# Slice 0's long convolution filter transformed earlier, its first shift's last two additions moved to accumulating DMAs, in the backward pass of a gated block

## The chip, the cores and the metric

The kernel runs on 1 core of a Trainium2 chip. A core has a matrix engine (TensorE, PE in the profile), a vector engine (VectorE, DVE), a scalar/activation engine (ScalarE, ACT), a general engine (GpSimd, POOL) and a queue engine (SyncE, SP). DMAs are issued from SP, ACT and POOL, each into a queue of its own, and all run on the core's 16 DMA engines. The metric is the device time of one execution in microseconds (us); lower is better.

## What is computed

The reference runs a forward pass and its gradients with respect to nine inputs. S = 2048 rows, D = 1024 columns, F = 3584.

```python
    def _A_ref(q, k, v, shift_k, ssm_k, ssm_D):
...
        k_pad = jnp.pad(k, ((0, 0), (ks - 1, 0), (0, 0)))
        k_shift = jnp.zeros_like(k)
        for t in range(ks):
            k_shift = k_shift + k_pad[:, t:t + S, :] * shift_k[:, ks - 1 - t][None, None, :]
        kv = k_shift * v
...
        y_f = kv_f * kf_f[None, :, :, :]
        y = (lambda x, s, axes=(-2,-1): jnp.fft.irfft2(x, s=s, axes=axes).astype(jnp.bfloat16))(y_f, (1, L), axes=(1, 2))[:, 0, :S, :]
        y = y + kv * ssm_D[None, None, :]
        return q * y

    def _B_ref(x, w_gate, w_up, w_down):
        g = jnp.einsum("bsd,df->bsf", x, w_gate)
        u = jnp.einsum("bsd,df->bsf", x, w_up)
        h = g * u
        return jnp.einsum("bsf,fd->bsd", h, w_down)

    x = A_q
    xn = _layernorm(x, axis=-1)
    s = _A_ref(xn, A_k, A_v, A_shift_k, A_ssm_k, A_ssm_D)
    g = _silu(_B_ref(xn, B_w_gate, B_w_up, B_w_down))
    return x + s * g
```

The outputs are `out` and the gradients of `sum(out * grad_out)`. Part A is a four-tap causal shift of k, a product with v, and a long causal convolution (by Fourier transforms of length 2S) with the filter `ssm_k`. Part B is a gated linear unit.

## The kernel before

**Stages.** From 0 to about 50 us the rows of x are normalized (six chunks of 1, 1, 2, 4, 4 and 4 row blocks, list `chunks`), transposed into `XNT` and, chunk by chunk, multiplied with the first weight slabs. Until about 500 us the gate and up products of all 14 slabs run on PE (`gu_unit`), and in between the forward convolution of part A. Then follow the down projection, the gate with silu, the backward convolution and the weight gradients.

**A unit of the gate and up products.** `gu_unit(sl, b0, n, w, tick)` (L658) takes one slab of 256 + 256 weight columns and n row blocks. For each block it issues 8 matmuls of 512 columns into a PSUM tile `psg` (L676), a cast by ACT into `gut` (L678), and a call of `tick`. The product of gate and up, `hN`, is made by DVE in the next unit (L687), stored by POOL (`Hd<-hN`) and transposed by PE some blocks later. Slabs are loaded by SP (`load_slab`, L546, two DMAs of 512 KB, L550) into the tile `wslab`, which has two buffers: slab 2 can only be loaded when the last unit of slab 0 is done, slab 3 after slab 1.

**The convolution as a generator.** `conv_forward` (L745) yields the estimated DVE time of each piece. `make_pump` (L469) runs it up to a given share of `F_TOTAL`, and `tick` (L1019) calls the pump after every row block, so that the pieces are spread over the units. It works on 8 slices of 128 columns. Pairs of slices share k and v: `load_kv` (L748) loads them, by POOL, into `krow` and `U[4]`; `shift` (L765) makes the four-tap shift of pair 0 and the product kv, `shift_later` (L784) that of pairs 1 to 3. In `shift` DVE makes 4 products, 3 additions and the product with v, 8 instructions of about 2.3 us. In `shift_later` the 3 additions are DMAs issued by POOL that add `U[7]` to `U[6]` (L794). POOL then stores the shift (`KSHd`).

For slice 0 come, in this order: `shift(0)`, the transposes of the filter rows (`h_rows`, L800), two halves of the filter's transform on PE and ACT (`half`, L848, with `fwd8_half`, L286), the butterflies of the filter's transform on DVE (`transform`, L855, with `fwd8`, L296, in six steps), within them the two halves of kv's transform (`ahead`), the butterflies of kv's transform, their product and the inverse transform. `fwd8(..., late=True)` calls `ahead(0)` after its second and `ahead(1)` after its third step behind the sums.

**Tables.** The transforms multiply with two tables of sines and cosines, `T4[0]` and `T4[1]` (in the tile `TF`). `angles` (L154, POOL) makes the integer angles `m` and `mm`, `mask_angles` (L168, DVE) reduces them, `build_tables` (L175, ACT) makes sine, absolute value and sine for each table, and `turn_tables` (L185) transposes both into the tile `TI`. Slice 0's transforms (`fwd8_half`) read only `T4[0]`; `T4[1]` is first read by `turn_tables`.

**What sets the order.** Instructions are traced in program order and then ordered on each engine by a scheduler, in the order of tracing among those that it takes for ready. An instruction that is ready early can go ahead of others that were traced before it. Two means hold it: `tc.issue_after(x)` queues a block's instructions behind x on x's engine, and `tc.keep_in_program_order` puts an instruction behind everything traced on its engine so far (all DVE instructions made by `tt` and `stt` once `PIN[0]` is set, and the first matmul of each part of a held half transform). The loads of k and v of pair 0 stand in a block behind the row store of chunk 4 (`issue_after(xsts[4].ins)`). On its engine each instruction runs in the order so fixed.

**Where the pieces stand.** The last units of slabs 0 and 1 are written by (slab, chunk): (0,4), (0,5), (1,4), (1,5). The pump starts after (0,5). `cnt` counts blocks from -5: the filter rows are transposed from the first block of (1,4) on (`cnt == -4`), the filter's halves and the rest from its third block on (`cnt >= -2`).

Of the kernel before, what the change touches and what calls it, by code (L numbers as in the profile page):

```python
# [19 lines left out]
def build_kernel(  # L20
# [12 lines left out]
    P = 128  # L33
# [120 lines left out]
    def angles(tg):  # L154
# [9 lines left out]
        mm = tg.tile([P, 8, P], I32, name="mm1")  # L164
        E.iota(mm[:], pattern=[[512, 8], [0, P]], base=0, channel_multiplier=0)
        return (m, mm), ins

    def mask_angles(ang):  # L168

        m, mm = ang  # L170
        tt(mm[:], m[:], mm[:], ADD)
        for x in ang:
            V.tensor_single_scalar(x[:], x[:], 4095, ALU.bitwise_and)

    def build_tables(tg, ang):  # L175

        for q, mm in enumerate(ang):
            dst = T4[q].rearrange("p r k f -> p k r f")
            sc = 2.0 * np.pi / 4096.0
            nc.scalar.activation(dst[:, 1], mm[:], ACT.Sin, bias=negpi[:], scale=sc)  # L180
            ab_ = tg.tile([P, 8, P], F32, name="ab_")
            nc.scalar.activation(ab_[:], mm[:], ACT.Abs, bias=negpi[:], scale=sc)
            nc.scalar.activation(dst[:, 0], ab_[:], ACT.Sin, bias=mhpi[:], scale=1.0)
# [555 lines left out]
    SHIFT_W = 8 * 2.3  # L739
# [5 lines left out]
    def conv_forward():  # L745
        S_ = conv_state

        def load_kv(dp, c):  # L748
            S_["k", dp] = krow
            if dp > 1 and c == 0:  # L750
                load_taps(WB[:, :, dp % 2], dp * 256, 256)
            if dp > 0 or c == 0:
                for i in range(2) if dp == 0 else (c,):
                    cld_k(krow[:, i], i, dp)
            if dp > 0 or c == 1:
                for i in range(2) if dp == 0 else (c,):
                    v = U[4][:, 2048 * i:2048 * i + 2048].rearrange("p (a x) -> p a x", a=8)
                    cld_v(v, i, dp * 256, 256)
# [6 lines left out]
        def shift(dp):  # L765
            kv = cx.tile([P, NB, 256], BF16, name="kv")
            S_["kvt", dp] = kv
            k = S_.pop(("k", dp))
            wb = lambda j: WB[:, j:j + 1, dp % 2].unsqueeze(1).to_broadcast([P, 2, 8, 256])
            room = cx.tile([P, 16, 256], BF16, name="KX")[:].rearrange("p a x -> p (a x)") if dp == 0 else U[7][:]  # L770
            acc, prod, v = [t.rearrange("p (c r d) -> p c r d", c=2, r=8) for t in (U[6][:], room, U[4][:])]
            with tc.issue_after(last.ins):
# [1078 lines left out]
```

## Time and profile before

| | us |
|---|---|
| median of 3 runs | 1908.7 (1908.37 to 1909.15) |
| the profiled execution | 1907.69 |
| its span | 1905.9 |
| granted TensorE clock | 1.0 throughout |

The span is the time from the first to the last instruction in the profile. Busy times are of instructions on an engine; matmuls are pipelined, so that their records overlap. Around the change the profile has these times (us from the span's start):

| what | start | end |
|---|---|---|
| last k of pair 0 issued by POOL | 38.7 | |
| v of pair 0 issued, four DMAs | 39.8 | |
| first product of the shift on DVE | 50.03 | 52.3 |
| third addition of the shift | 64.94 | 67.2 |
| product kv | 67.27 | 69.6 |
| table 1 made on ACT (three instructions) | 60.30 | 64.5 |
| k of pair 1 issued from | 65.2 | |
| filter's half transforms on PE | 68.35 | 71.6 |
| filter's sums on DVE | 71.00 | 75.6 |
| filter's third step behind the sums, end | | 83.6 |
| kv's half transforms on PE | 72.97 | 77.2 |
| table transposes on PE, first and second | 89.94 and 101.64 | |

Slab loads to landing took 3.9 to 35.8 us, accumulating DMAs of 1 MB 8.2 to 12.4 us.

### The profile page before, as it was taken

Reading aid. Unit: us, or ns where it says so; the run is one execution under the profiler, and the core shown is the slowest. Engines: PE = TensorE matmul, PEld = TensorE weight load, DVE = VectorE, ACT = ScalarE, POOL = GpSimd, SP = SyncE. Lnnn points to the kernel's source line nnn. Section 1 sums busy time; section 2 is a strip of 40 time slices with the busy share of each in tenths; the row PEclk is TensorE's granted clock in tenths of the full one; section 3 lists DMA queues with packets and bytes.
Section 4 is the critical chain, followed back from the end, with each engine's and each line's share of the span. In section 5 each row is a group of like instructions: output and inputs, shape, how many; then the busy total and the mean of one; then the engine's idle time right before and its main releaser. Section 6 shows DMA issues by size and latency. Waiting matters only on the chain.

```text
span 1905.9 us, 28127 instructions
## 1 busy us (share of the span) xinstructions
PE 1895.9 (99%) x11363; PEld 1012.1 (53%) x11363; DVE 1541.4 (81%) x1726; ACT 636.9 (33%) x928; POOL 348.1 (18%) x479
## 2 busy tenths in 40 slices
PE   8999999999999999999999999999999999999999
PEld 5555555555444466666666655664444444444444
DVE  8999999999977546887999999999995305788872
ACT  5755555555332234332222222222222102011121
POOL 5213122111013210001121221211212101111120
PEclk9999999999999999999999999999999999999999
DMA  9989878888769996677897799585877999899862
GB/s 298 311 249 302 262 243 266 249 284 278 253 219 313 302 328 227 210 231 235 252 283 237 238 252 267 191 283 172 240 230 190 227 201 199 173 185 194 189 182 102
DMA packets 428562, 454.82 MB, mean 239 GB/s; under 512 B 268656, under 2 KB 343692, under 8 KB 414096
## 3 DMA queue, kind: packets, MB, share of 16 engines
q1 hardware_dynamic: 355504, 226.97, 44.7%
q0 software_dynamic: 43936, 184.11, 31.5%
q10 hardware_dynamic: 28992, 41.95, 6.2%
q8 instruction: 89, 1.46, 0.3%
q14 instruction: 41, 0.34, 0.1%
HBM read 194.92 MB, written 189.84 MB: 202 GB/s over the span
## 4 chain that ended last, share of the span: by engine, by line
PE 97%; DVE 1%; ACT 1%; DMA 0%; SPq 0%; issue 0%
PE psb L1538 20%; PE psx L1683 20%; PE psg L676 19%; PE psb L1521 10%; PE psbm L1069 10%; PE psb L1621 9%; PE psF L233 3%; PE psI L454 1%; PE tr L568 1%; PE psY L1228 1%; PE psY L444 1%; PE psx L1621 1%; DVE bst L581 0%; DMA wslab<-in_B_w_gate_dram 0%; PE tr L811 0%; PE psY L1621 0%
## 5 line engine op out<-in xcount | busy, mean ns | idle before, releaser
L676 PE MATMUL psg<-wslab,U 128*128 128x512 bf16 x1792 | 403.0, 379 | 3.4 <-DMA wslab<-in_B_w_gate_dram 2.0
L1538 PE MATMUL psb<-U,U 128*128 128x512 bf16 x1792 | 397.1, 379 | 0.0
L1683 PE MATMUL psx<-U,dgut 128*128 128x512 bf16 x1536 | 332.8, 379 | 0.0
L1683 PEld LDWEIGHTS <-dgut 128*128 128x128 bf16 x1792 | 175.3, 98 | 211.4
L1538 PEld LDWEIGHTS <-U 128*128 128x128 bf16 x1792 | 175.3, 98 | 197.9
L676 PEld LDWEIGHTS <-U 128*128 128x128 bf16 x1792 | 172.0, 98 | 195.7 <-issue 3.6
L1521 PE MATMUL psb<-wdt,U 128*128 128x256 bf16 x1792 | 205.6, 273 | 0.0
L211 DVE TENSOR_TENSOR W<-W 128x1024 f32<-128x1024 f32 (+1 forms) x195 | 191.7, 998 | 4.2
L1521 PEld LDWEIGHTS <-U 128*128 128x128 bf16 x1792 | 175.2, 98 | 29.2
L1621 PE MATMUL psb<-U,U 128*128 128x512 bf16 x816 | 177.3, 379 | 0.0
L1543 ACT CAST wb<-psb 128x512 bf16<-128x512 f32 x112 | 65.6, 586 | 315.4 <-PE psb L1538 310.5
L1288 DVE SCALAR_TENSOR_TENSOR dkp<-dkT,kT 128x1024 bf16<-128x1024 bf16 (+2 forms) x64 | 78.3, 1224 | 100.1 <-DMA dkT<-DKSHd 98.4
L1069 PE MATMUL psbm<-U,ht 128*128 128x512 bf16 x672 | 146.0, 379 | 0.0
L1621 PEld LDWEIGHTS <-U 128*128 128x128 bf16 x912 | 88.9, 98 | 103.1
L1715 ACT ACTIVATE dx_t<-dxn 128x1024 bf16<-128x1024 f32 x15 | 15.9, 1057 | 324.0 <-DVE dxn L211 324.0
L678 ACT CAST gut<-psg 128x512 bf16<-128x512 f32 x144 | 84.4, 589 | 112.2 <-PE psg L676 110.0
L1069 PEld LDWEIGHTS <-ht 128*128 128x128 bf16 x672 | 65.6, 98 | 78.1
L211 DVE TENSOR_TENSOR U<-U,dht 128x2048 bf16<-128x2048 bf16 x56 | 68.3, 1220 | 47.1 <-ACT dht L1523 47.0
L1523 ACT CAST dht<-psb 128x512 bf16<-128x512 f32 x112 | 65.6, 587 | 116.4 <-PE psb L1521 116.4
L66 POOL DMA_DIRECT2D Hd<-hN x54 | 38.8, 719 | 246.7 <-DVE hN L211 243.4
L1662 ACT CAST wbs<-psb 128x512 bf16<-128x512 f32 x51 | 29.9, 586 | 145.4 <-PE psb L1621 137.3
L211 DVE TENSOR_TENSOR W<-SP 128x1024 f32<-128x1024 f32 x64 | 74.3, 1219 | 2.6 <-ACT SP L255 1.2
(266 smaller groups left out, 2351.1 us busy)
## 6 DMA issues: line engine op xcount, KB each, us to landing
U<-GUd SPq DMA_DIRECT2D x28, 1024.0 KB, 9.9
DGd<-U SPq DMA_DIRECT2D x28, 1024.0 KB, 6.8
GUd<-gut ACTq DMA_DIRECT2D x36, 512.0 KB, 7.6
out_dram<-wb SPq DMA_DIRECT2D x112, 128.0 KB, 5.3
U<-Hd SPq DMA_DIRECT2D x14, 1024.0 KB, 5.8
Hd<-hN POOLq DMA_DIRECT2D x54, 256.0 KB, 6.5
HTd<-hT ACTq DMA_DIRECT2D x24, 512.0 KB, 5.5
U<-U POOLq DMA_DIRECT2D x9, 1024.0 KB, 11.7
```

The costliest lines, as they stand in the source:

```text
L211: pinned(V.tensor_tensor(o, a, b, op))
L233: mm = nc.tensor.matmul(ps[:, k].rearrange("p (c d) -> p c d", c=2), T[:, r, k, :], xr[:, r], start=(n == 0), stop=(n == len(rs) - 1 and ( ...
L676: gu_mm[0] = nc.tensor.matmul(ps[:], XNT[q][:, dc, qi * P:(qi + 1) * P], w[:, dc].rearrange("p a f -> p (a f)"), start=(dc == 0), stop=(dc ...
L678: nc.scalar.copy(out=gut[:, :, i], in_=ps[:].rearrange("p (a f) -> p a f", a=2))
L1069: mm = nc.tensor.matmul(ps[:, dh * 512:(dh + 1) * 512], ht(fc)[:, i * P:(i + 1) * P], WD[fc // 4][:, fc % 4, dh * 512:(dh + 1) * 512], sta ...
L1288: ins = V.scalar_tensor_tensor(prod[:].rearrange("p r d -> p (r d)")[:, lo:H], dkT[:, 0, lo:H], 1.0, kT[:, 0, 13 + m + lo:13 + m + H], op0 ...
L1521: nc.tensor.matmul(ps[:, x * SLW:(x + 1) * SLW], DBMT[2 * hf + g][:, dc, (b % 4) * P:(b % 4 + 1) * P], wdt[:, dc, :], start=(dc == 0), sto ...
L1523: nc.scalar.copy(out=dht[:, 2 * e:2 * e + 2].rearrange("p b f -> p (b f)"), in_=ps[:])
L1538: nc.tensor.matmul(ps[:], XN[b // 4][:, b % 4, dc * P:(dc + 1) * P], dgus[b // 8][:, :, b % 8], start=(b == 0), stop=(b == NB - 1))
L1543: nc.scalar.copy(out=wb[:, dc % 2].rearrange("p a f -> p (a f)"), in_=ps[:])
L1621: nc.tensor.matmul(ps, h[:, f, b, :], DBM[b // 4][:, b % 4, dh * 512 + d0:dh * 512 + d0 + w], start=(b == 0), stop=(b == NB - 1))
L1683: nc.tensor.matmul(ps[:, dh * 512:(dh + 1) * 512], t[n][:, f, i * P:(i + 1) * P], WGU[n][:, f, dh * 512:(dh + 1) * 512], start=(n == 0 and ...
```

## The change

- `shift(0)` is replaced by `first_shift` and `first_kv`. DVE makes the four products (into `U[6]`, `KX`, `U[7]` and a buffer of `HX`) and one addition. The third and the fourth product are added into `U[6]` by accumulating DMAs, each in two halves of 512 KB, issued by POOL.
- v of pair 0 is no longer loaded in the block behind chunk 4's row store: `load_v(0)` is called after the first pair of accumulating DMAs.
- The product kv and the store `KSHd[0]` (`first_kv`) are made when the filter's transform calls `ahead(1)`, and both halves of kv's transform behind them; before, the halves stood at `ahead(0)` and `ahead(1)`.
- The next pair's `load_kv` and `shift_later` for slice 0 are traced after the filter's transform (`load_next(0)`).
- `build_tables` becomes `build_table`: table 0 is built where both were built, table 1 behind the filter's half transforms. The angles `mm` and the second `ab_` lie in `TI`.
- The pump starts before unit (0,5). `cnt` starts at -9; the filter rows are transposed after the second block of (0,5), the rest from its fourth block on. `F_TOTAL` and the shift's share (`SHIFT0_W`) are smaller.

```diff
@@ -161,26 +161,24 @@
         m = tg.tile([P, 8, P], I32, name="m")
         ins = E.tensor_tensor(m[:], f2[:].unsqueeze(1).to_broadcast([P, 8, P]),
                               tcol[:].unsqueeze(2).to_broadcast([P, 8, P]), ALU.mult)
-        mm = tg.tile([P, 8, P], I32, name="mm1")
-        E.iota(mm[:], pattern=[[512, 8], [0, P]], base=0, channel_multiplier=0)
-        return (m, mm), ins
+        mm = TI[:, 0].rearrange("p r k f -> p (r k f)").bitcast(I32).rearrange("p (r f) -> p r f", r=8)
+        E.iota(mm, pattern=[[512, 8], [0, P]], base=0, channel_multiplier=0)
+        return (m[:], mm), ins
 
     def mask_angles(ang):
 
         m, mm = ang
-        tt(mm[:], m[:], mm[:], ADD)
+        tt(mm, m, mm, ADD)
         for x in ang:
-            V.tensor_single_scalar(x[:], x[:], 4095, ALU.bitwise_and)
-
-    def build_tables(tg, ang):
-
-        for q, mm in enumerate(ang):
-            dst = T4[q].rearrange("p r k f -> p k r f")
-            sc = 2.0 * np.pi / 4096.0
-            nc.scalar.activation(dst[:, 1], mm[:], ACT.Sin, bias=negpi[:], scale=sc)
-            ab_ = tg.tile([P, 8, P], F32, name="ab_")
-            nc.scalar.activation(ab_[:], mm[:], ACT.Abs, bias=negpi[:], scale=sc)
-            nc.scalar.activation(dst[:, 0], ab_[:], ACT.Sin, bias=mhpi[:], scale=1.0)
+            V.tensor_single_scalar(x, x, 4095, ALU.bitwise_and)
+
+    def build_table(q, mm, ab_):
+
+        dst = T4[q].rearrange("p r k f -> p k r f")
+        sc = 2.0 * np.pi / 4096.0
+        nc.scalar.activation(dst[:, 1], mm, ACT.Sin, bias=negpi[:], scale=sc)
+        nc.scalar.activation(ab_, mm, ACT.Abs, bias=negpi[:], scale=sc)
+        nc.scalar.activation(dst[:, 0], ab_, ACT.Sin, bias=mhpi[:], scale=1.0)
 
     def turn_tables(psp):
 
@@ -736,7 +734,7 @@
     ht_st = [None]
     EIGHT = ((0, 0), (0, 1), (3, 0), (5, 0), (6, 0), (7, 0), (7, 1))
     INV8 = (2, 4, 5, 6, 7)
-    SHIFT_W = 8 * 2.3
+    SHIFT_W, SHIFT0_W = 8 * 2.3, 5 * 2.3
 
     conv_state = {"forward": True, "filters": True}
 
@@ -744,42 +742,52 @@
 
     def conv_forward():
         S_ = conv_state
+
+        def load_v(dp, cs_=(0, 1)):
+            for i in cs_:
+                cld_v(U[4][:, 2048 * i:2048 * i + 2048].rearrange("p (a x) -> p a x", a=8), i, dp * 256, 256)
 
         def load_kv(dp, c):
             S_["k", dp] = krow
             if dp > 1 and c == 0:
                 load_taps(WB[:, :, dp % 2], dp * 256, 256)
-            if dp > 0 or c == 0:
-                for i in range(2) if dp == 0 else (c,):
-                    cld_k(krow[:, i], i, dp)
-            if dp > 0 or c == 1:
-                for i in range(2) if dp == 0 else (c,):
-                    v = U[4][:, 2048 * i:2048 * i + 2048].rearrange("p (a x) -> p a x", a=8)
-                    cld_v(v, i, dp * 256, 256)
+            for i in range(2) if dp == 0 else (c,):
+                cld_k(krow[:, i], i, dp)
+            if dp > 0:
+                load_v(dp, (c,))
 
         def load_h(ds):
             hrow = U[5][:, 0:2048].rearrange("p (c u r) -> p c u r", c=2, r=8)
             cld(U[5][:, 0:2048], A_ssm_k[ds * P:(ds + 1) * P, :])
             S_["h", ds] = hrow
 
-        def shift(dp):
+        def first_shift():
             kv = cx.tile([P, NB, 256], BF16, name="kv")
-            S_["kvt", dp] = kv
-            k = S_.pop(("k", dp))
-            wb = lambda j: WB[:, j:j + 1, dp % 2].unsqueeze(1).to_broadcast([P, 2, 8, 256])
-            room = cx.tile([P, 16, 256], BF16, name="KX")[:].rearrange("p a x -> p (a x)") if dp == 0 else U[7][:]
-            acc, prod, v = [t.rearrange("p (c r d) -> p c r d", c=2, r=8) for t in (U[6][:], room, U[4][:])]
-            with tc.issue_after(last.ins):
-                tt(acc, k[:, :, 0:8, :], wb(3), MUL)
-            yield 2.3
-            for j in (2, 1, 0):
-                tt(prod, k[:, :, 3 - j:11 - j, :], wb(j), MUL)
+            S_["kvt", 0] = kv
+            k = S_.pop(("k", 0))
+            wb = lambda j: WB[:, j:j + 1, 0].unsqueeze(1).to_broadcast([P, 2, 8, 256])
+            rooms = [U[6][:], cx.tile([P, 16, 256], BF16, name="KX")[:].rearrange("p a x -> p (a x)"), U[7][:],
+                     cs.tile([P, 16, 256], BF16, name="HX", bufs=2)[:].rearrange("p a x -> p (a x)")]
+            terms = [t.rearrange("p (c r d) -> p c r d", c=2, r=8) for t in rooms]
+
+            for i, j in enumerate((3, 2, 1, 0)):
+                with tc.issue_after(last.ins) if i == 0 else nullcontext():
+                    tt(terms[i], k[:, :, 3 - j:11 - j, :], wb(j), MUL)
                 yield 2.3
-                tt(acc, acc, prod, ADD)
-                yield 2.3
-            tt(kv[:].rearrange("p (c r) d -> p c r d", c=2), acc, v, MUL)
-            st(KSHd[dp], U[6][:].rearrange("p (b d) -> p b d", b=NB))
-            yield 2.3
+                if i == 1:
+                    tt(rooms[0], rooms[0], rooms[1], ADD)
+                    yield 2.3
+                for c in range(2) if i > 1 else ():
+                    nc.gpsimd.dma_start(out=rooms[0][:, 2048 * c:2048 * c + 2048], in_=rooms[i][:, 2048 * c:2048 * c + 2048],
+                                        accum_op=ADD, max_dma_last_dim=4096)
+                if i == 2:
+                    load_v(0)
+
+        def first_kv():
+            v, acc = [U[i][:].rearrange("p (c r d) -> p c r d", c=2, r=8) for i in (4, 6)]
+            tt(S_["kvt", 0][:].rearrange("p (c r) d -> p c r d", c=2), acc, v, MUL)
+            st(KSHd[0], U[6][:].rearrange("p (b d) -> p b d", b=NB))
+            pe_us[0] -= 2.3 / 0.95
 
         def shift_later(dp):
             kv = cx.tile([P, NB, 256], BF16, name="kv")
@@ -836,8 +844,6 @@
                 yield
 
         load_kv(0, 0)
-        yield 0.0
-        load_kv(0, 1)
         yield 0.0
         cx = pool("cx", 1)
         cs = pool("cs", 1)
@@ -879,7 +885,7 @@
             step()
             yield net(2.4)
 
-        yield from shift(0)
+        yield from first_shift()
         PIN[0] = True
         yield 3.9
         h_rows(0, 0)
@@ -887,13 +893,22 @@
         yield 0.1
         tl = turn_tables(ps_cv)
         sp = [half(0, S_["hx"], i, Dz[:, 0:P]) for i in range(2)]
+        build_table(1, ang[1], TI[:, 1].rearrange("p r k f -> p (r k f)").bitcast(F32).rearrange("p (r f) -> p r f", r=8))
+
+        def first_halves(i):
+            if i == 1:
+                first_kv()
+                sph.extend(half(0, kvs(0), i) for i in range(2))
+
+        def load_next(ds):
+            with tc.issue_after(S_["kst"].ins) if ds else nullcontext():
+                for c in range(2):
+                    load_kv(ds // 2 + 1, c)
+            return shift_later(ds // 2 + 1)
         for ds in range(8):
             yield 0.5
-            if ds % 2 == 0 and ds < 6:
-                with tc.issue_after(S_["kst"].ins) if ds else nullcontext():
-                    for c in range(2):
-                        load_kv(ds // 2 + 1, c)
-                later_kv = shift_later(ds // 2 + 1)
+            if ds in (2, 4):
+                later_kv = load_next(ds)
             D0 = Dz[:, ds * P:(ds + 1) * P]
             sph = []
             KX = cx.tile([P, 16, 256], BF16, name="KX")
@@ -901,7 +916,8 @@
             own_room = lambda X: X[:].rearrange("p a x -> p (a x)").bitcast(F32).rearrange("p (a x) -> p a x", a=8)[:, 0:4]
             eight = (ds, 1) in EIGHT
             if ds == 0:
-                yield from transform(0, 1, sp, HX, own_room(KX), lambda i: sph.append(half(0, kvs(0), i)), nop)
+                yield from transform(0, 1, sp, HX, own_room(KX), first_halves, nop)
+                later_kv = load_next(0)
             else:
                 yield from transform(ds, 0, sp, KX, own_room(HX), lambda i: sph.append(half(ds, S_["hx"], i, D0)), nop)
                 S_["kst"] = st(KFd[ds], KX[:])
@@ -957,7 +973,7 @@
         kst.release()
 
     F_TOTAL = 4 * SHIFT_W + 3.0 + 8 * (0.5 + FWD4_W + 1.3 + PROD_W + INV_W) + 10.0 - 0.95 * 8 * (4 * 1.75 + 0.95 + 4 * 0.9)
-    F_TOTAL -= 3 * 3 * 2.3
+    F_TOTAL -= (3 * 3 + 2) * 2.3
     F_TOTAL += len(EIGHT) * (FWD8_W - 9.6 + 0.95 * 1.75) - 2.0
     F_TOTAL += len(INV8) * (INV8_W - INV_W + 0.95 * 1.8)
     conv = conv_forward()
@@ -994,17 +1010,16 @@
                 spread_taps()
         if i == 3:
             with tc.issue_after(xsts[4].ins):
-                for _ in range(2):
-                    next(conv)
+                next(conv)
         if i == 4:
             with tc.issue_after(act_copy[0].ins):
                 nc.scalar.activation(Dz[0:1, :], Dz[0:1, :], ACT.Copy, scale=WSC)
-        for i_, sl in ([(0, 0)], [(1, 0), (0, 1), (1, 1)], [(2, 0), (2, 1)], [(3, 0), (3, 1)], [(4, 0)], [(5, 0)])[i]:
+        for i_, sl in ([(0, 0)], [(1, 0), (0, 1), (1, 1)], [(2, 0), (2, 1)], [(3, 0), (3, 1)], [(4, 0)], [])[i]:
             gu_unit(sl, *xs[i_][0:2], slabs[sl], nop)
         if i == len(xs) - 1:
             with tc.issue_after(root.ins), tc.issue_after(last.ins):
                 mask_angles(ang)
-                build_tables(tg, ang)
+                build_table(0, ang[0], tg.tile([P, 8, P], F32, name="ab_")[:])
     chunk[0] = len(xs)
     st(RSd.rearrange("(c u r) -> u c r", c=2, u=P), RSTD[:].rearrange("u (c r) -> u c r", c=2))
     st(RSTN[:], RSd.rearrange("(b p) -> p b", p=P))
@@ -1013,19 +1028,19 @@
     ps_st[1].release()
     ps_cv = pool("ps_cv", 2, space=PSUM)
     pump, drain, step = make_pump(conv, F_TOTAL)
-    cnt = [-5]
+    cnt = [-9]
     NT = 24 * 8.0 + 33
 
     def tick(by=1):
         cnt[0] += by
-        if cnt[0] == -4:
-            pump((SHIFT_W + 4.05) / F_TOTAL)
-        if cnt[0] >= -2:
-            pump((SHIFT_W + (F_TOTAL - SHIFT_W) * (cnt[0] + 6.5) / (NT + 3.5)) / F_TOTAL)
-
-    pump((SHIFT_W + 3.95) / F_TOTAL)
-    for i_ in (4, 5):
-        gu_unit(1, *xs[i_][0:2], slabs[1], tick)
+        if cnt[0] == -7:
+            pump((SHIFT0_W + 4.05) / F_TOTAL)
+        if cnt[0] >= -5:
+            pump((SHIFT0_W + (F_TOTAL - SHIFT0_W) * (cnt[0] + 9.5) / (NT + 6.5)) / F_TOTAL)
+
+    pump((SHIFT0_W + 3.95) / F_TOTAL)
+    for sl, i_ in ((0, 5), (1, 4), (1, 5)):
+        gu_unit(sl, *xs[i_][0:2], slabs[sl], tick)
     for sl in range(2, NSL - 2):
         w, wld = load_slab(sl, nc.sync)
         for hf in range(2):
```

## The prediction

> **What bounds the kernel now.** First the page's busy times:
>
> ```profile
> PE 1895.9 (99%) x11363; PEld 1012.1 (53%) x11363; DVE 1541.4 (81%) x1726; ACT 636.9 (33%) x928; POOL 348.1 (18%) x479
> ```
>
> TensorE (PE) works 1895.9 of 1905.9 us. So the sum below only asks which PE waits go and which come. The waits of PE, all of them over 0.2 us in total:
>
> ```profile
> PE psg L676 <- DMA wslab<-in_B_w_gate_dram: 2.0, 2, 1.5
> PE tr L527 <- POOL ident masks.py:199: 1.4, 1, 1.4
> PE psg L676 <- ACT gut L678: 1.1, 2, 0.9
> PE tr L568 <- DVE U L600: 0.7, 1, 0.7
> PE tr L617 <- DVE U L600: 0.5, 1, 0.5
> ```
>
> In the timeline all but 0.2 us of these lie before 40 us (the last at 74.3), ahead of the first instruction that the change reorders on PE. Busy time by stretches confirms it:
>
> ```profile
> 60.00:70.00 10.00, 10.00 (x69) 5.78 (x68) 9.93 (x6) 8.38 (x12) 3.50 (x6) 1.00 0.77 218
> 70.00:80.00 10.00, 9.79 (x63) 5.64 (x61) 9.12 (x11) 9.91 (x14) 5.37 (x7) 1.00 1.02 358
> 80.00:90.00 10.00, 10.00 (x55) 4.79 (x54) 9.90 (x15) 4.28 (x7) 1.37 (x2) 1.00 1.08 357
> ```
>
> The columns are the stretch, its length, then PE, PE's loads, DVE, ACT, POOL, clock (1.00), DMA share and GB/s. PE is full; DVE and the DMA engines are nearly full too, so what is taken from DVE and laid on the DMA engines matters only through a PE wait. One input of PE has little room here, the weight slab. In the timeline of the SP queue:
>
> ```profile
> 62.81 0.37 SPq L550 DMA_DIRECT2D wslab<-in_B_w_up_dram  x1
> 63.24 0.57 SPq L550 DMA_DIRECT2D wslab<-in_B_w_gate_dram  x1
> 82.78 0.37 SPq L550 DMA_DIRECT2D wslab<-in_B_w_up_dram  x1
> ```
>
> There are two slab buffers. Slab 2 can be loaded when PE has left slab 0 (62.8), and slab 3's issue at 82.78 marks that PE has left slab 1: from 82.7 on PE needs slab 2. The load (2 x 512 KB) has 20 us. It took 8.1 us (63.24 to landing), but the same load elsewhere did not:
>
> ```profile
> DMA to landing us min/median/max: 3.9/7.7/35.8
> ```
>
> The DMA queues in three windows tell when. First 64 to 68 us, slab 2's load beside an almost silent POOL queue (q0; SP's is q1, ACT's q10):
>
> ```profile
> q1 hardware_dynamic: 1704, 0.86, 75.3%
> q0 software_dynamic: 80, 0.26, 16.9%
> ```
>
> then 268 to 273 us, a slab load beside one accumulating DMA:
>
> ```profile
> q0 software_dynamic: 240, 0.98, 97.6%
> q1 hardware_dynamic: 161, 0.08, 7.8%
> ```
>
> then 156 to 187 us, a slab load behind the end of an accumulation and beside POOL's next loads of k and v and its stores:
>
> ```profile
> q0 software_dynamic: 1762, 7.00, 63.8%
> q10 hardware_dynamic: 1985, 2.98, 26.8%
> q1 hardware_dynamic: 2016, 1.02, 11.3%
> ```
>
> So the slab moves at 0.86/4 = 0.215 MB/us with POOL's queue quiet, at 0.08/5 = 0.016 beside an accumulation, at 1.02/31 = 0.033 beside POOL's other traffic.
>
> **The change, part by part.**
>
> *Two additions off DVE.* Two TENSOR_TENSOR of 2.29 us (59.81, 64.94) go: 4.6 us of DVE, which ends no PE wait here: 0. Four products and one addition end at about 62.1 (before: the second addition's end) instead of 67.2.
>
> *Accumulation by DMA.* Four DMAs of 512 KB instead, on POOL. A 1 MB one (L794) holds POOL 1.22 us, a plain 1 MB store 0.54, so half lies between 0.3 and 1.2 each; I take 0.8, 3.2 us in all; POOL has room (3.50 of 10 busy). On the DMA engines 111 to 117 us shows 1.01 MB in 6 us at 98.2%, so 2.1 MB hold them 12.5 us. The third product ends at 59.8, the first bytes move 1.8 us after an issue (109.67; the window from 111 has them at 111.45), so at 61.6, and the last ends at 74.1 alone, about 75 with its 2 to 10% taken by others. The second pair is issued only when the first has landed; behind it on POOL wait the hN stores, the next k and KSHd. hN has three buffers, 7 us apart, so DVE does not feel it: 0.
>
> *Slice 0's filter sooner.* Its transposes, half transforms and DVE steps move 3 ticks forward; a tick is 8 matmuls of 216 ns (32 in 6.91 us), 5.2 us together. PE issues the same matmuls: 0. The gain is at most the waits after 36 us: 0.9 (39.5) and 0.2; the first is in front of the change, so I take 0.2, bounds 0 and 1.1. The product kv now stands on DVE behind the third step of the filter: that step ended at 83.6, now 78.4. Accumulated by 75, kv does not wait: 0. If it does, the last two filter steps and hN queue behind it on DVE and PE's half transforms of kv behind them (a rival).
>
> *Second half of the tables.* Three ACT operations of 1.16 + 1.17 + 1.18 = 3.5 us move from 60.3 to behind the filter's PSUM copies. Their first reader is the second transpose group (101.6, now some 5 us sooner), 20 us later: 0. Without that cover PE would wait up to 3.5.
>
> *v.* Its four loads (3.2 us of POOL, landed by some 11 us) lose their place in the held block. They wait for nothing but U4, free since about 31, so they are issued beside k as now, needed at 78: 0. Behind the first pair they cost the second pair 1 MB/0.3 = 3.4 us (2.33 MB in 40 to 50 us at 81.7%).
>
> *The rest.* Unit (5,0) behind the pump keeps its PE place, so slab 0 is still left at 62.4; `mm` and the second `ab_` only lie in TI, first written by the table transposes at 91.3; the next pair's k loads, traced later now, are ready when the fourth product has read `krow` (62.1, before 64.9), its v when kv has read U4 (80.7, before 69.6; used at 163): 0 each.
>
> *What the accumulation does to slab 2.* This is the term. Before, POOL's queue was silent from 60 to 66 and the slab used it. Now accumulations fill 61.6 to 75. The slab gets (75-64) x 0.016 = 0.18 of its 1.05 MB. Then the queue holds k of slice pair 1 (1.4 MB), KSHd (1.05), the next filter rows (0.5) and two hN (0.5), 3.5 MB at the 156 to 187 rate 7.00/31 = 0.226: 15.5 us, in which the slab gets 0.51 MB; the rest 0.36/0.215 = 1.7 us. Landing 75 + 15.5 + 1.7 = 92.2 against 82.7: 9.5 us of PE. From whole loads instead: gate landed 20.4 us after issue with one accumulation just ahead (115.31), 35.8 at 153.14 (accumulation, then k, KSHd and v, in the order that this stretch gets): 63.2 + 20.4 = 83.6 and 99.0, a wait of 0.9 to 16.3, middle 8.6. I take 7.0, under the middle, since POOL's own waits (the second pair, KSHd behind the last pair) leave its queue gaps that I cannot place, and each us of silence is worth 0.215 MB; both ends, and 0, stay for the range.
>
> The Trainium skill (DMA: Bandwidth & Descriptors, "Queues, rings and completion order") says that each DMA engine serves its queues in turn, a packet of some 9 to 17 descriptors at a time. By that the slab would get about half of the engines beside an accumulation, by my estimate land near 74, and not be missed. The 7.8% row speaks against it; its result is the second rival.
>
> **Sum.** Profiled execution 1907.7 (span 1905.9): +7.0 -0.2 = 1914.5. The median of the runs shown, 1908.7, is 1.0 above that execution; so 1915.5.
>
> **Rivals.** (1) Likeliest: slab 2 late, chance 0.56, own range 1909.5 to 1925; 0.08 of it stays below +3.8. (2) *Not slower*: POOL's queue falls silent, or the queues share evenly, so that 3.5 to 4 us of free engines (0.87 MB/0.215) fall between 75 and 82.7. For it: POOL is held at the second pair and at KSHd; against it: k (1.4 MB) is ready at 62 and was issued in that very place at 149.99, beside the accumulation. If the slab lands by 82.7, nothing is paid: 1908.7 - 0.2 = 1908.5; chance 0.20. (3) kv late: v is issued behind the first pair, the second pair ends at 75 + 3.4, shared with others until 84; PE reaches kv's halves at about 81 (78.4 + 2.3): +3 to 5, 1913; for it: v is traced there; against it: v is ready 30 us sooner; chance 0.12, and it exceeds 3.8 in most of it. (4) The change does not do what it says: v, held by nothing, goes ahead of k; k lands (49.7) up to 3.4 later, the chain starts later, slab 2 gets 63.9 to 65 free, 0.24 MB: 7.0 - 0.24/0.033 < 0, about +1: 1910; chance 0.07. (5) Faster by over 3.8 would need waits to go that lie before 40 us, where nothing is moved: 0.05 with all I overlook, 1904.5.
>
> **Numbers.** About 0.2% (3.8 us) is what a measurement here can tell from no change. Slower: 0.48 + 0.12 = 0.60; within: 0.08 + 0.20 + 0.07 = 0.35; faster 0.05. Range 1907.5 to 1923: it leaves out (5), the low edge of (2) and the landings beyond 35.8 - 2 us.
>
> **What would show it.** PE's waits gain a row psg <- wslab of some 7 us near 83; slab 2's gate lands 20 to 36 us after its issue; q1's share is below a tenth from 64 to 75; DVE does not wait for U<-U before kv; the second table half ends before 80; no wait at psT. Wrong if PE stays full from 60 to 100, or if its wait is at kv's halves instead.

## The result: 1914.3 us

| | us | runs |
|---|---|---|
| before | 1908.78 median (1907.92 to 1909.41) | 8 |
| changed | 1914.28 median (1912.54 to 1917.08) | 8 |
| ratio | 1.0031, 95% interval 1.0021 to 1.0041 | |
| profiled execution, changed | 1912.76, span 1911.0 | |

The change made the kernel 5.5 us slower; the two profiled executions lie 5.1 us apart. The three longest runs of the changed kernel (1915.69 to 1917.08) show a mean granted clock of 0.999, the other five 1.000. The forecast was 1915.5 (1907.5 to 1923), slower. So the time came out as said. The reason did not: PE never waited for slab 2.

### Where the 5 us lie

The page's line of busy times of the changed kernel:

```profile
PE 1889.5 (99%) x11227; PEld 1012.0 (53%) x11363; DVE 1538.2 (80%) x1724; ACT 636.8 (33%) x928; POOL 352.9 (18%) x483
```

TensorE (PE) still bounds. 136 matmul records are missing in this trace (11227 of 11363), so PE's busy time can't be compared; its weight loads (PEld) are complete in both. Setting the n-th load of one trace against the n-th of the other, the changed kernel is 0.3 us behind at 49 us, up to 4.6 us behind around 100 us and 5.1 us behind at the end: nearly all of the loss lies between 50 and 100 us. The waits of PE in the changed kernel (total, times, longest):

```profile
PE psg L674 <- ACT gut L676: 2.8, 2, 1.9
PE psg L674 <- DMA wslab<-in_B_w_gate_dram: 2.0, 2, 1.0
...
PE psF L231 <- DVE kv L209: 1.3, 1, 1.3
...
PE tr L725 <- DVE hN L209: 0.7, 1, 0.7
```

The slab row is that of the kernel's first microseconds, as before. New are 1.9 for a cast, 1.3 for kv and 0.7 for hN. PE's timeline says where (start, length, and in brackets the idle time ahead of it):

```profile
68.42 3.61 PE L674 MATMUL psg<-wslab,U 128*128 128x512 bf16 x16 [1.88 <-ACT gut L676]
72.73 0.40 PE L725 MATMUL tr<-ident,hN 128*128 128x128 bf16 x4 [0.70 <-DVE hN L209]
...
81.08 1.03 PE L231 MATMUL psF<-kv,TF 128*128 128x256 bf16 x8 [1.25 <-DVE kv L209]
```

Three waits, 3.8 us together, all between 66 and 82 us, where the moved pieces stand; before, this stretch had one of 0.20 us. About 1 us of the loss shows in no wait. The granted clock is 1.00 from 50 to 100 us. Each wait has its own cause. ScalarE (ACT):

```profile
63.07 3.77 ACT L292 COPY SP<-psF 128x1024 f32<-128x1024 f32 x4
66.69 1.20 ACT L180 ACTIVATE TI<-TI,negpi 128x1024 f32<-128x1024 int32 x1
67.74 0.62 ACT L676 CAST gut<-psg 128x512 bf16<-128x512 f32 x1
```

The cast that frees PE's PSUM bank stands behind the filter's four PSUM copies and a step of table 1. Before, casts stood behind the same four copies too, here ACT and then PE:

```profile
69.04 3.76 ACT L294 COPY SP<-psF 128x1024 f32<-128x1024 f32 x4 [0.77 <-PE psF L233]
72.66 1.06 ACT L729 COPY hT<-tr 128x1024 bf16<-128x1024 bf16 x1
73.56 1.13 ACT L678 CAST gut<-psg 128x512 bf16<-128x512 f32 x2
```

```profile
72.97 1.04 PE L233 MATMUL psF<-kv,TF 128*128 128x256 bf16 x8
...
74.26 1.89 PE L676 MATMUL psg<-wslab,U 128*128 128x512 bf16 x8 [0.20 <-ACT gut L678]
```

There PE had the first half of kv's transform to do while ACT copied, and waited 0.20 us. In the changed kernel kv's halves come only at 81 us, and between the filter's halves and the wait PE has no more than two gate or up matmuls and eight transposes. That kv's halves had covered the copies is read from these orders; no run puts them back there. VectorE (DVE):

```profile
65.05 4.63 DVE L209 TENSOR_TENSOR W<-SP 128x1024 f32<-128x1024 f32 x4 [2.88 <-ACT SP L292]
...
71.99 0.69 DVE L209 TENSOR_TENSOR hN<-gut 128x1024 bf16<-128x1024 bf16 x1
...
78.73 2.29 DVE L209 TENSOR_TENSOR kv<-U,U 128x4096 bf16<-128x4096 bf16 x1 [1.11 <-DMA U<-HX]
```

hN stands behind the filter's sums and the two steps behind them (before, hN ran at 69.48 and the sums at 71.00), and kv waits for the last accumulating transfer. GpSimd (POOL) shows why that comes late:

```profile
59.95 1.83 POOL L781 DMA_DIRECT2D U<-U  x2 [1.54 <-PE psg L674]
66.37 0.85 POOL L781 DMA_DIRECT2D U<-HX  x1 [4.58 <-issue]
68.98 0.85 POOL L781 DMA_DIRECT2D U<-HX  x1 [1.77 <-DMA U<-U]
...
78.99 0.56 POOL L66 DMA_DIRECT2D KSHd<-U  x1 [7.87 <-DMA U<-HX]
```

The second pair goes out only when the first has landed, half by half, and ends at 78.7. And the slab (first the transfers issued from 62.5 to 75 us, with the time from issue to landing, then SP's timeline):

```profile
wslab<-in_B_w_up_dram SPq DMA_DIRECT2D x1, 512.0 KB, 6.4
wslab<-in_B_w_gate_dram SPq DMA_DIRECT2D x1, 512.0 KB, 17.0
```

```profile
66.55 1.34 SPq L548 DMA_DIRECT2D wslab<-in_B_w_gate_dram  x1
...
87.93 0.37 SPq L548 DMA_DIRECT2D wslab<-in_B_w_up_dram  x1
```

Issued at 66.55, landed 17.0 us later at 83.6 (before: 8.1 us): slowed as forecast. But the issue of slab 3 at 87.93 shows that PE came to slab 2 only then, 5.1 us later than before, 4.4 us after it had landed.

### The profile page after: what moved, and what is told of

The parts are those of the page before. It is cut to its first block, busy times and chain, and to the rows that moved or that the text cites. A ratio compares the mean times of both kernels' runs of the same rounds, so it can differ in the third digit from the quotient of the medians.

```text
span 1911.0 us, 27994 instructions
## 1 busy us (share of the span) xinstructions
PE 1889.5 (99%) x11227; PEld 1012.0 (53%) x11363; DVE 1538.2 (80%) x1724; ACT 636.8 (33%) x928; POOL 352.9 (18%) x483
## 4 chain that ended last, share of the span: by engine, by line
PE 96%; DMA 2%; DVE 1%; ACT 1%; issue 1%; SPq 0%; POOLq 0%
PE psb L1553 20%; PE psx L1698 20%; PE psg L674 18%; PE psb L1536 10%; PE psbm L1084 10%; PE psb L1636 9%; PE psF L231 3%; PE psI L452 1%; PE tr L566 1%; PE psY L1243 1%; PE psY L442 1%; PE psx L1636 1%; DMA U<-HX 1%; DVE bst L579 0%; DMA wslab<-in_B_w_gate_dram 0%
## 5 line engine op out<-in xcount | busy, mean ns | idle before, releaser
L674 PE MATMUL psg<-wslab,U 128*128 128x512 bf16 x1731 | 398.4, 379 | 8.5 <-ACT gut L676 2.8
```

What stands on the lines that cost most here:

```text
L674: gu_mm[0] = nc.tensor.matmul(ps[:], XNT[q][:, dc, qi * P:(qi + 1) * P], w[:, dc].rearrange("p a f -> p (a f)"), start=(dc == 0), stop=(dc ...
```

## The experiments

All times are medians; "before" ran beside each kernel and lay between 1908.53 and 1908.81.

| label | us | ratio, 95% interval |
|---|---|---|
| changed | 1914.28 | 1.0021 to 1.0041 |
| e1_table_back | 1913.40 | 1.0014 to 1.0032 |
| e2_halves_later | 1911.41 | 1.0004 to 1.0022 |
| e3_adds_on_dve | 1914.37 | 1.0017 to 1.0037 |
| e4_pump_late | 1919.20 | 1.0035 to 1.0060 |
| e5_table_late | 1915.32 | 1.0023 to 1.0047 |
| e6_both_later | 1910.72 | 1.0001 to 1.0018 |
| e7_pump_late_hT | 1913.17 | 1.0016 to 1.0043 |
| e8_filter_tick_later | 1911.03 | 1.0003 to 1.0020 |
| e9_old_order_no_accum | 1910.83 | 1.0003 to 1.0021 |
| e10_old_order_one_accum | 1910.45 | 1.0000 to 1.0018 |
| e11_one_accum_table_back | 1911.07 | 1.0003 to 1.0022 |

Four theories of where the loss comes from went into the runs. **A**: the three waits stand in series; in PE's fixed order, now with the filter ahead and both of kv's halves behind its third step, what ends last (kv) sets their sum. **B**: the waits, that of the cast behind table 1 first, are losses of their own. **D**: the accumulating transfers cost it. **P**, the prediction's: slab 2 is late.

### e1, e2, e3, e4: one part each

```diff
 # e1
                 build_table(0, ang[0], tg.tile([P, 8, P], F32, name="ab_")[:])
+                build_table(1, ang[1], TI[:, 1].rearrange("p r k f -> p (r k f)").bitcast(F32).rearrange("p (r f) -> p r f", r=8))
...
-        build_table(1, ang[1], TI[:, 1].rearrange("p r k f -> p (r k f)").bitcast(F32).rearrange("p (r f) -> p r f", r=8))
 # e2
                 first_kv()
-                sph.extend(half(0, kvs(0), i) for i in range(2))
...
                 yield from transform(0, 1, sp, HX, own_room(KX), first_halves, nop)
+                sph.extend(half(0, kvs(0), i) for i in range(2))
 # e3, in first_shift
-                if i == 1:
-                    tt(rooms[0], rooms[0], rooms[1], ADD)
+                if i > 0:
+                    tt(rooms[0], rooms[0], rooms[i], ADD)
                     yield 2.3
-                for c in range(2) if i > 1 else ():
-                    nc.gpsimd.dma_start(out=rooms[0][:, 2048 * c:2048 * c + 2048], in_=rooms[i][:, 2048 * c:2048 * c + 2048],
-                                        accum_op=ADD, max_dma_last_dim=4096)
...
-    SHIFT_W, SHIFT0_W = 8 * 2.3, 5 * 2.3
+    SHIFT_W, SHIFT0_W = 8 * 2.3, 7 * 2.3
-    F_TOTAL -= (3 * 3 + 2) * 2.3
+    F_TOTAL -= 3 * 3 * 2.3
 # e4: unit (5,0) ahead of the pump again, counts as before the change
-    cnt = [-9]
+    cnt = [-5]
...
-    for sl, i_ in ((0, 5), (1, 4), (1, 5)):
-        gu_unit(sl, *xs[i_][0:2], slabs[sl], tick)
+    for i_ in (4, 5):
+        gu_unit(1, *xs[i_][0:2], slabs[1], tick)
```

> The changed kernel with the second half of the tables built where it was, right behind the first half and ahead of the pump. In the profile of the changed kernel PE waits three times between 60 and 85 us: 1.88 us for the cast of gut (ACT stands at four PSUM copies and one table operation), 0.70 us for hN, 1.25 us for kv. Theory A (the waits stand in series, and what sets their sum is the time at which kv is ready for its half transforms): the wait for the cast shrinks by the table operation of 1.2 us, the later ones grow by as much, the time stays within 0.7 us of the changed kernel. Theory B (ACT's queue is a loss of its own): 1.2 to 1.9 us faster than the changed kernel. Theory P (the prediction: the weight slab comes late): no change.

> The changed kernel with the two half transforms of kv traced behind the filter's whole transform instead of behind its third step, so that PE comes to them some units later. Theory A: PE no longer waits for kv (1.25 us) and has 2 ticks more room, 1.2 to 3.5 us faster than the changed kernel, unless the weight slab, which landed 4.4 us before PE needed it, then becomes the next wait. Theory B: 1.25 us faster at most, with the 1.88 us wait for the cast untouched. Theory P: no change.

> The changed kernel with all three additions of the first shift on DVE again and no accumulating DMA there; the order of the pump, of v, of the tables and of kv behind the filter's third step stays. DVE ends the shift 4.6 us later, POOL's queue has no accumulation. Theory A: kv is made at the time that DVE's own chain gives, about 79 to 81 us instead of 78.7; within 1.5 us of the changed kernel. Theory D (the accumulating DMAs themselves cost the time, by kv's wait and by their share of the DMA engines): 2 us or more faster than the changed kernel, near the kernel before. Theory P: the slab lands within 10 us of its issue.

> The changed kernel with the pump started behind unit (0,5) again and its counts as before, so that filter and kv reach PE at the old blocks, 5.2 us later; the accumulating DMAs, the moved table and kv behind the third step stay. Theory A: PE reaches kv's halves after kv is ready: no wait over 0.5 us from 60 to 100 us, time back to the kernel before within 1 us. Theory P (slab 2 starved by the accumulations): slab 0 is left at 62.4 us again while the accumulations fill 61 to 78 us, so a wait for the slab of 1 to 9 us near 83 us, time as long as that of the changed kernel or longer. Theory D: at least 1 us slower than the kernel before.

**e1**: 1913.40, 0.9 less than changed. PE's timeline of e1:

```profile
60.78 0.22 PE L817 MATMUL tr<-ident,U 128*128 128x128 bf16 x1 [1.13 <-ACT hx L820]
...
62.73 0.77 PE L725 MATMUL tr<-ident,hN 128*128 128x128 bf16 x8 [1.29 <-ACT hx L820]
...
88.25 3.61 PE L674 MATMUL psg<-wslab,U 128*128 128x512 bf16 x16 [0.89 <-DMA wslab<-in_B_w_gate_dram]
```

The cast's wait is gone, but the table now delays the copies of the filter's rows (2.4 us), and slab 2, issued at 70.3 here, is 0.9 us late. ACT is busy for 18.7 of the 20 us from 50 to 70; moving its steps about moves the wait.

**e2**: 1911.41, 2.9 less. kv's wait is gone, the other two are what they were (1.88 and 0.70 us in PE's timeline), and DVE's wait for the transfers in front of kv, now 3.6 us, costs nothing since PE has other work. More than kv's 1.25 us is gained in the medians. The two profiled executions (1912.76 and 1911.61), both at full clock, lie 1.15 us apart, which is kv's wait; what adds the rest to the medians no trace shows.

**e3**: 1914.37, as changed. With no accumulating transfer at all:

```profile
68.43 3.61 PE L674 MATMUL psg<-wslab,U 128*128 128x512 bf16 x16 [1.26 <-ACT gut L676]
74.09 0.61 PE L725 MATMUL tr<-ident,hN 128*128 128x128 bf16 x4 [2.05 <-DVE hN L209]
```

The two additions push the filter's sums back on DVE by 1.4 us (66.41 instead of 65.05), and the wait moves from kv, and in part from the cast, to hN. So D's forecast fails: without the transfers nothing is won. But e3 brings 4.6 us of additions back to DVE, and does not price the transfers by themselves. Nor is slab 2 quick without them: its last packet starts 15.4 us after the issue (66.14 to 81.6), since POOL's queue now carries the next k and KSHd in their place.

**e4**: 1919.20, a miss: slower than the change itself. ACT's timeline, and the queues from 61 to 68 us (packets, MB, share of the engines):

```profile
70.95 1.02 ACT L820 ACTIVATE hx<-tr 128x1024 bf16<-128x1024 bf16 x1 [7.10 <-DMA HTd<-hT_s]
```

```profile
q0 software_dynamic: 324, 1.17, 80.0%
q10 hardware_dynamic: 250, 0.48, 18.5%
q1 hardware_dynamic: 139, 0.14, 7.2%
```

In this order the copy of the filter's rows is written over memory that a store of the last unit (HTd<-hT_s, issued by SP at 60.84) still reads. Before, that store had landed 3 us after its issue (60.45 to 63.40). Here the accumulations on POOL's queue (q0) hold the engines, SP's queue (q1) gets 7.2%, the store lands 10.0 us after its issue, and PE waits 7.1 us for the copy. So starvation of SP's queue is real, but e4 does not show the order alone.

### e5, e6, e8: are the waits losses of their own, or do they stand in series?

```diff
 # e5: table 1 behind the filter's transform
-        build_table(1, ang[1], TI[:, 1].rearrange("p r k f -> p (r k f)").bitcast(F32).rearrange("p (r f) -> p r f", r=8))
...
                 yield from transform(0, 1, sp, HX, own_room(KX), first_halves, nop)
+                build_table(1, ang[1], TI[:, 1].rearrange("p r k f -> p (r k f)").bitcast(F32).rearrange("p (r f) -> p r f", r=8))
                 later_kv = load_next(0)
 # e6: e2 and e5;  e8: e6 and
-        if cnt[0] >= -5:
+        if cnt[0] >= -4:
```

> The changed kernel with one edit: the last two ScalarE steps of table 1 traced behind the filter's whole transform, so that the cast at 67.74 us no longer stands behind one of them. Theory A, waits in series: kv is finished at 81.0 us whatever TensorE does before, because it waits for the accumulating transfers (landed 78.70). The 1.9 us that the cast no longer costs come back in front of kv's halves, whose wait grows from 1.25 to about 3.1 us: 1914.3 us, as changed. Theory B, each wait is a loss of its own: the 1.9 us are saved, kv's wait stays 1.25: about 1912.4.

> e2 (kv's halves behind the filter's whole transform, 1911.4 us) and the edit of e5 together. Theory A: the cast's wait of 1.88 us goes, but the next thing in TensorE's order is the transposes of hN, and hN stands on VectorE behind the filter's first steps, which end at 72.5 us whatever TensorE does: the wait for hN grows from 0.70 to about 2.6, and the time stays 1911.4. Theory B: 1909.5. The prediction's theory: TensorE now comes to slab 2 up to 4 us sooner than in the changed kernel, near 83.5 us, while it landed at 80.6 to 83.1 us in the runs so far: a wait on the slab of 0 to 3 us.

> e6 with the steps of the filter's transform let in one tick later (from count -4 instead of -5), so that VectorE does the product hN ahead of the filter's sums. Theory A: the last of the three waits goes, none takes its place, since kv's halves stand late enough: 1909 us within 0.7. Theory B: as e6 less 0.7, about 1908.8. So A and B are told apart by e5 and e6; this run tells whether the three waits are the whole loss. If 1911 or more is left, something else costs, above all slab 2, which TensorE now needs near 83 us.

**e5**: 1915.32, not 1912.4. PE and DVE of e5:

```profile
67.07 10.52 PE L674 MATMUL psg<-wslab,U 128*128 128x512 bf16 x48 [0.84 <-ACT gut L676]
...
83.36 1.86 PE L231 MATMUL psF<-kv,TF 128*128 128x256 bf16 x8 [4.25 <-DVE kv L209]
```

```profile
81.02 2.29 DVE L209 TENSOR_TENSOR kv<-U,U 128x4096 bf16<-128x4096 bf16 x1 [3.71 <-DMA U<-HX]
```

The cast's wait fell from 1.88 to 0.84 and hN's went, and kv's wait grew from 1.25 to 4.25 us. Theory A holds here and B falls: what PE saves ahead of kv's halves it waits there. The wait grew by more than was saved, because the second pair landed at 81.0 instead of 78.7; it was issued 0.7 and 1.1 us later (67.06 and 70.05). The medians of e5 and changed lie 1.0 us apart, within their intervals.

**e6**: 1910.72, between the two forecasts. Its forecast by A rested on hN standing next on PE, but in e6's order 48 matmuls stand there instead, as in e5, and no wait for hN came. Left are 0.84 us for the cast and 0.89 for kv, although kv's halves stand later.

**e8**: 1911.03. PE's next wait:

```profile
83.39 0.38 PE L674 MATMUL psg<-wslab,U 128*128 128x512 bf16 x1 [1.24 <-DMA wslab<-in_B_w_gate_dram]
```

kv no longer waits, but now the slab does: PE comes to it at 82.1 and waits 1.24 us. This is the prediction's wait, at its place, once most of the others in front of it are gone (0.84 us for the cast is left). The three waits were thus not the whole loss; they hid a fourth.

### e7, e9, e10, e11: before's order of the filter

```diff
 # e7: e4, and the transposed tile in the room of the later units
-            hT = fg.tile([P, 4, 2, 2, P], BF16, name="hT", bufs=2)[:, 0:2] if chunk[0] > 5 else lnp.tile([P, 2, 2, 2, P], BF16, name="hT_s", bufs=5)[:]
+            hT = fg.tile([P, 4, 2, 2, P], BF16, name="hT", bufs=2)[:, 0:2] if chunk[0] > 4 else lnp.tile([P, 2, 2, 2, P], BF16, name="hT_s", bufs=5)[:]
 # e9: e7 and e3 (no accumulating transfer)
 # e10: e7, only the last addition by accumulating transfers
+                if i in (1, 2):
+                    tt(rooms[0], rooms[0], rooms[i], ADD)
+                    yield 2.3
+                for c in range(2) if i > 2 else ():
 # e11: e10 and e1
```

> e4 (all of the change but the place of the filter) with the transposed tile of unit (0,5) taken from the room that the later units use, so that the copy of the filter's rows does not lie on memory that a store on SP's queue still reads. Theory A and B: the accumulating transfers, the table behind and v behind k cost nothing by themselves; no wait over 0.5 us on TensorE between 55 and 100 us, 1908.8 us within 1 us. Prediction's theory: slab 2 (issued near 63 us) competes with the accumulations and is needed near 83 us: it lands after 83, 1910 to 1916.

> e7 (before's order of the filter; 1913.2 us, TensorE waits 4.7 us for slab 2 at 81.9 us) with all three additions on VectorE, so that of the change only the table behind and v behind k are left. If the accumulating transfers made slab 2 late: slab 2, issued near 63 us, lands by 76 us, no wait for it, 1908.8 us within 1 us. If v behind k, or anything else on GpSimd's queue, does it: the wait for slab 2 stays at 2 us or more, 1911 to 1913.

> e7 with half the dose: the second addition on VectorE, only the last one by accumulating transfers (1 MB instead of 2). If the accumulations make slab 2 late by their bytes: it lands between e9's time and e7's, some 75 to 79 us, and that is before it is needed near 82: no wait, 1908.8 us within 1 us. If one pair is enough to hold it: a wait of 1 to 4 us, 1910 to 1913.

> e10 (before's order of the filter, one addition by accumulating transfers; 1910.45 us against 1908.56 of before, TensorE waits 0.99 us for a cast at 72.1 us that stands on ScalarE behind table 1's last step and the filter's PSUM copies) with table 1 built right behind table 0, as before the change. If the place of the table is what is left: no wait for that cast, 1908.6 us within 0.7. If v behind k or the accumulating transfers cost something that no wait on TensorE shows: 1910 or more. Below 1908 it would be the faster of all, which nothing so far points to.

**e7**: 1913.17, by the prediction's theory. PE's timeline, the slab's landing, and the queues from 74 to 78 us:

```profile
86.62 5.70 PE L674 MATMUL psg<-wslab,U 128*128 128x512 bf16 x13 [4.74 <-DMA wslab<-in_B_w_gate_dram]
```

```profile
wslab<-in_B_w_gate_dram SPq DMA_DIRECT2D x1, 512.0 KB, 22.8
```

```profile
q0 software_dynamic: 213, 0.81, 101.4%
q1 hardware_dynamic: 103, 0.05, 5.2%
```

Slab 2, issued at 63.66, lands 22.8 us later, and PE waits 4.7 us for it near 82. Nine tenths of its packets had started by 73.7; the rest is held while POOL's queue has all of the engines. (This execution took 1917.8; e7's runs reach from 1911.05 to 1920.46, so the median one loses less.) The Trainium skill (DMA: Bandwidth & Descriptors, "Queues, rings and completion order") has the engines serve their queues in turn, a packet at a time. Turns of unequal packets are no equal shares of time: in this row POOL's queue has 213 packets of 3.8 KB on average and SP's 103 of 0.5 KB, two to one in number and some twenty to one in time. In number the turns can come out even, as in the changed kernel from 77 to 80 us:

```profile
q0 software_dynamic: 181, 0.62, 54.7%
q10 hardware_dynamic: 179, 0.36, 30.9%
q1 hardware_dynamic: 181, 0.17, 17.0%
```

There the trace agrees with the rule. Why SP's queue got only half as many turns from 74 to 78 us in e7, no run shows.

The wait also cost more than itself. PE came back at 86.6, and not at full clock (PE's busy time, then the granted clock, DMA share and GB/s):

```profile
85.00:90.00 5.00, 3.38 (x9) 0.56 1.03 383
90.00:95.00 5.00, 4.98 (x29) 0.76 1.05 333
```

The trace has the granted clock at 0.5 from 85.6 to 92.4; by my estimate that took 2.9 us of PE's work. The other traces show the same: 3.4 us at 0.5 in e1 (from 63.0, behind waits of 1.1 and 1.3 us), in e3 (from 74.1, behind 2.0 us) and in e5 (from 82.8, within the 4.2 us), and 10.2 us in e4 (from 67.7, within the 7.1 us). In changed, e2, e6 and e8 to e11, where no wait of this stretch is over 1.9 us, the clock stays at 1.00. So the times of e1, e3, e4, e5 and e7 hold lost clock beside the waits.

**e9, e10**: the dose. The queues from 64 to 69 us, first of e7, then of e9:

```profile
q0 software_dynamic: 248, 0.86, 79.4%
q1 hardware_dynamic: 336, 0.29, 18.6%
```

```profile
q1 hardware_dynamic: 1731, 0.89, 68.0%
q0 software_dynamic: 54, 0.15, 10.8%
```

Without the accumulations (e9) SP's queue moves 0.89 MB in the same 5 us, three times as much, the slab's last packet starts at 72.3, and PE doesn't wait for it. With one pair (e10) it is the same (0.84 MB, last packet at 71.0), since that pair is issued at 65.3, behind the slab. So in this order it is the accumulating transfers that make slab 2 late (e3 showed that other transfers on POOL's queue do it too). Whether half the bytes or the later issue helped, e10 does not tell; in e11, with the pair 0.4 us sooner, the slab's last packet starts only at 76.3. But both kernels miss the 1908.8: 1910.83 and 1910.45. One wait of 0.99 us in each, for the cast behind table 1 and the filter's copies, shows (here e9):

```profile
72.75 5.34 PE L674 MATMUL psg<-wslab,U 128*128 128x512 bf16 x24 [0.99 <-ACT gut L676]
```

**e11**: 1911.07, a miss: the table's place is not what is left. That wait is gone, and waits of 0.64 (for the copy hT) and 0.38 us (for kv) come in its place.

From e9 to e3 only the filter and the pump that holds it move ahead (and unit (0,5) has its transposed tile elsewhere), with all additions on DVE in both: 1910.83 to 1914.37, **3.5 us**, in which e3's profiled execution has 1.7 us of lost clock. From e9 to e7 only the accumulations come, in the old order: **2.3 us**. In the new order, trading two additions on DVE for them changes nothing (e3 and changed). What is left between before and e9 to e11, 1.9 to 2.3 us, is placed in part only. Of the change these keep v behind k, and also kv and both its halves behind the filter's third step, which e9's forecast overlooked; e9 and e10 keep table 1 behind too. In e9 and e10 the cast's wait is 0.8 us longer than the 0.20 of before, where PE had kv's halves to do. No run puts the halves back, so their price and the rest stay open. None of the versions is faster than before.

## Why the forecast was right in time and wrong in reason

**Slab 2 late, +7.0: the step that failed.** In the changed kernel it cost nothing. Of the signs that the prediction named, four failed: there was no wait for the slab near 83, the slab landed after 17.0 us instead of 20 to 36, SP's queue had 41.8% from 64 to 74 us instead of under a tenth, and DVE did wait for an accumulation in front of kv (1.11 us). One of its signs of being wrong, a wait at kv's halves, came. The times can occur: in e7 the slab took 22.8 us from issue to landing. But the rate of 0.016 was that of a load's end, used for a whole load. By the trace of before, 1823 of that load's 2048 packets had started from 260 to 268 us, ahead of the 7.8% row, and the 5.2% row of e7 is the end of slab 2 in the same way. The order of events failed too. I let the accumulations run without a gap from 61.6 to 75 and put 3.5 MB of POOL's other transfers right behind them. But POOL held the second pair until the first had landed, and KSHd until 79.0. In the gaps between them nine tenths of the slab had started by 74.2; only the last tenth was held back, to 83.1. And I set 82.7 as the time of need while PE lost 5 us before it. Where it loses less (e8, e7) the wait is there, 1.2 and 4.7 us, the size of the lower half of the 0.9 to 16.3. The half of the engines that I worked out from the rule of turns was a misreading: turns of 0.5 KB against 3.8 KB give SP's queue far less than half of the time.

**"PE issues the same matmuls: 0."** Wrong, and the main cost: 2.6 us for the cast and hN in the changed kernel, 3.5 us from e9 to e3. The matmuls are the same, but what stands beside them is not: four PSUM copies of 0.94 us in front of a cast, with kv's halves gone that PE had worked on meanwhile, and the sums of 4.6 us in front of hN. I had looked at what the moved steps do on PE and not at what they stand in front of on the other two engines.

**"kv does not wait: 0."** Wrong: 1.25 us, as the accumulations ended at 78.7, not 75. This is rival 3 (0.12), with its place (PE at kv's halves near 80) and its cause, the second pair, but not its price (3 to 5 us); there v was to be the reason, and v had landed by 63.6.

**The second half of the tables, 0.** The first reader was indeed far off. But the cover I named was the wrong one: behind the step on ACT stood the cast. Yet e1, e5 and e11 give no more than 0.9 us back for moving it.

**Two additions off DVE, 0; issue on POOL, 3.2 us, 0.** No run speaks against it: e3, with the additions back on DVE, is no faster than the change, and the four issues took 1.83 + 0.85 + 0.85 = 3.5 us.

**Rival 2** (POOL's queue falls silent at the second pair and at KSHd, 0.20) had the right mechanism for the slab and the wrong time, since it knew no other wait. **v, 0**: it was not issued beside k (36.8 to 40.1) but from 46.8 to 57.7, still in time. No run moved it alone; what is left in e9 and e11, 2.3 us, is the most that it can cost there.

So the right time came by luck from a wrong sum: +7.0 for a wait that did not come, nothing for three that did.

## What to carry to other kernels

When a block of work is moved on a full engine, list for every other engine what now stands behind the moved block's helpers, and who needs that first; a step with its own reader far away still delays its neighbours. Waits in a fixed order are not summed: taking one away shows the next (cast, then kv, then the slab), so a wait of 1.9 us is worth what the next one leaves of it. Nor is a long wait worth only its length: look at the granted clock behind it. Keep long transfers on one queue well behind a load on another queue that has a due time.

## What the hardware showed

- A load on SP's queue beside accumulating transfers does not slow evenly: in the changed kernel 90% of its packets had started 8.1 us after the issue and the last only after 17.0; with POOL's queue almost silent (before) 90% took 5.9 and all 7.5.
- Halving an accumulating transfer did not halve its time to landing: the four of 512 KB took 5.9 to 9.7 us in the changed kernel, beside the 8.2 to 12.4 of those of 1 MB before.
- With three queues at work, each got the same number of packets (181, 179 and 181 in 3 us of the changed kernel) and shares of time in the order of their packets' sizes (54.7, 30.9 and 17.0%).
- Within or behind long waits of PE its granted clock stood at 0.5: for 3.4 us with 2.0 us of waiting (e3) and 4.2 (e5), 6.8 us with 4.7 (e7), 10.2 us with 7.1 (e4), and 3.4 us with two waits of 1.1 and 1.3 close together (e1). With 1.88 us (changed, e2) it did not fall.
- A store on the same queue is starved in the same way (10.0 us to landing in e4 instead of 3.0), and through the memory that it reads it holds up engines that have nothing to do with it (PE by 7.1 us).
